# Attention and MLP on one core: the second layer of batches 2 and 3 as seven block products for two row tiles, with all sums on VectorE

## The chip, the cores and the metric

The kernel runs on one core of one Trainium2 chip. A core has TensorE (PE, matrix products, written to PSUM), VectorE (DVE), ScalarE (ACT), GpSimd (POOL) and SyncE (SP, which here only issues transfers), each with its own instruction queue that runs in order. The metric is device time in microseconds. Before the change three runs gave a median of 288.89 us (288.71 to 291.12).

## What is computed

```python
# q, k, v: (batch 4, heads 8, seq 768, head_dim 64), float32
k_chunks = k.reshape(B, H, 24, 32, D)                        # chunks of 32 keys
k_min, k_max = np.min(k_chunks, axis=3), np.max(k_chunks, axis=3)
ub = np.sum(np.maximum(q[..., None, :] * k_min, q[..., None, :] * k_max), axis=-1)
ub = np.where(causal_by_chunk, ub, -1e9)
top_chunks = np.argsort(ub, axis=-1)[..., -6:]               # each query keeps 6 chunks
scores = np.where(sel & causal, q @ k.T / sqrt(D), -1e9)
attn_out = softmax(scores) @ v
x = attn_out.transpose(0, 2, 1, 3).reshape(4, 768, 512)
xn = (x - mean(x)) / sqrt(var(x) + 1e-6) * g_ln              # over the last axis
out = x + np.maximum(xn @ w_ch1, 0.0) @ w_ch2                # 512 -> 2048 -> 512
```

So there is a chunk-selecting attention on each of 32 heads, then a layer norm, and a two-layer MLP with a residual on 3,072 rows.

## The kernel before

**Tiling.** Heads go in 16 pairs, `g` 0 to 15, four pairs to a batch. The 768 positions of a batch are six row tiles of 128; three row tiles make a half batch `(b, r)`. Attention works by pair (pairs 0 to 3 by pair and half batch), the MLP by half batch.

**Attention of a pair.** `ld`/`ldb` load keys and queries, `ldv` the values. `turn` transposes them (on PE for pairs 0 to 3, in blocks on DVE for the others). `kbound` takes each chunk's minimum and maximum (DVE), `kdiag` builds the right operand for the bounds (POOL from pair 4 on). `qhi`, `qlo`, `qrel` make the high and the low half of the scaled query and of its positive part, as float16 (ACT, DVE). `bounds` gives the upper bounds (PE), `select` finds the seventh largest of each row and makes a mask (DVE), `maskt` transposes it (PE), `mring` copies it from PSUM. The scores are one matmul whose operands hold the query or key of one head in 64 partitions and mask rows in the other 64. These operands lie in rings of four buffers, `QA`, `QB`, `KA`, `KB`. `kcopy` fills the key part. `qring` fills the query part: for pairs 0 to 3 by ACT out of PSUM, for pairs 4 to 15 by two transfers that SP issues (L267, L268). Then `smm` (scores, PE, L414), `sexp` (exponential, ACT, L422), `diag` (causal mask, POOL), `values` (PE, L445), `norm` and `pstat` (normalisation and statistics, DVE).

**MLP of a half batch.** `centre` (DVE, L487) writes `xc` = (x - mean) * g as float16. `rstd` puts 1/sqrt(var) aside, with the power on POOL. `xt` transposes `xc` by a transfer. `m1.b.r.m` is two of the sixteen hidden tiles of the first layer (PE, 8 matmuls of 384 columns, L513), `relu` takes them from PSUM to `hT` (ACT, in three places DVE). `m2.b.r.i.j` is a quarter of the second layer for row tile `i`: four of sixteen matmuls with `hT` as the weights and 512 columns of `w2b` (L538). `fin` multiplies by `rstd`, adds `x` (one DVE instruction, L547) and stores. The very last tile is split into 384 and 128 columns.

**Order.** One long list, `ORDER`, names every step; `fn.a.b@w` calls `fn(a, b)` with `w` in `other[0]`, which picks another engine or a number of keep-warm matmuls (`busy`, L117). Each engine runs its instructions in the order of that list. A step waits for its data, and for a buffer that it takes again: PSUM has four one-bank buffers (`ps_t`: transposes, bounds, values, second layer) and two of two banks (`ps_m`: scores and first layer).

The transfers all run on the core's 16 DMA engines; SP's queue issues in order, and POOL's issues the values and both weight matrices.

Of the kernel before, what the change touches and what calls it, by code (L numbers as in the profile page):

```python
# [19 lines left out]
def kernel(  # L20
# [10 lines left out]
    nc = tc.nc  # L31
# [228 lines left out]
    def qrel(g):  # L260
        qh, ql, rh, rl = (st[g][nm][:, P:] for nm in ("qh", "ql", "rh", "rl"))
        nc.vector.tensor_scalar_max(rh, qh, 0.0)
        nc.vector.scalar_tensor_tensor(rl, qh, 0.0, ql, op0=ALU.is_gt, op1=ALU.mult)

    def qring(g, i=None):
        if i is None:
# [71 lines left out]
    def select(g, i=None):  # L338
# [4 lines left out]
        if g >= HP:  # L343
            ubt = smp.tile([P, NT - 1, 2, NCH], F32, name="ubt", tag="ubt", bufs=1)
            ubm = smp.tile([P, NT - 1, 2, NCH], F32, name="ubm", tag="ubm")
            nc.vector.tensor_tensor(ubt, ub[:, :, 1], causf, ALU.add)
# [131 lines left out]

    def centre(b, r):
# [3 lines left out]
        for i in range(TR):  # L483
            nc.vector.bn_aggr(h["mv"][:, i, :], h["st"][:, i])
        for i in range(TR):
            xs = xh(b, r)[:, i].rearrange("p h d -> p (h d)")
            nc.vector.scalar_tensor_tensor(  # L487
# [39 lines left out]
    def last(b, r, i):  # L527
        return (b, r, i) == (B - 1, NR - 1, TR - 1)

    def m2(b, r, i, j):  # L530
# [3 lines left out]
        n, cs = 4, slice(0, DM)  # L534
        if last(b, r, i):
            n, cs = 8, slice(0, DM - P) if j < 2 else slice(DM - P, DM)
        for kt in range(n * j % KT2, n * j % KT2 + n):
            nc.tensor.matmul(  # L538
                h["yp", i][:, cs], h["hT"][:, kt, i * P:(i + 1) * P], w2b[:, kt, cs],
# [3 lines left out]
    def fin(b, r, i, e=None):  # L543
        h = hf[b, r]
        cs = (slice(0, DM), slice(0, DM - P), slice(DM - P, DM))[0 if e is None else 1 + e]
        ot = outp.tile([P, DM], F32, name="ot", tag="ot")
        nc.vector.scalar_tensor_tensor(  # L547
            ot[:, cs], h["yp", i][:, cs], h["rstd"][:, i:i + 1], xh(b, r)[:, i].rearrange("p h d -> p (h d)")[:, cs],
            op0=ALU.mult, op1=ALU.add,
        )  # L550
        s = TR * r + i
        nc.sync.dma_start(out[b, s * P:(s + 1) * P, cs], ot[:, cs])
# [4 lines left out]
        consts ld.0.0 rrows.0.0 rinit.0 ld.1.0 ld.2.0 warm.8 turn.0.qn.0 rrows.2.1@1 qpos.0.0 rrows.3.1 qring.0.0  # L557
        turn.0.kn.0 rinit.2 kbound.0.0 rinit.1 turn.1.qn.0 kcopy.0.0 ld.3.0 turn.1.kn.0 kbound.1.0 kdiag.0.0
        qring.1.0 rrows.1.0 rinit.3 turn.2.qn.0@3 ld.0.1 rrows.0.1 bounds.0.0@2 kdiag.1.0 rrows.1.1 qpos.1.0
        select.0.0 turn.2.kn.0 kcopy.2.0@1 kcopy.1.0 qpos.2.0 bounds.1.0@2 kbound.2.0 qring.2.0 maskt.0.0 select.1.0  # L560
# [130 lines left out]
```

## Time and profile before

| | us | share of the span |
|---|---|---|
| span of the profiled run | 288.7 | |
| PE busy | 271.7 | 94% |
| DVE busy | 211.8 | 73% |
| ACT busy | 180.8 | 63% |
| POOL busy | 94.1 | 33% |
| first layer on PE (L513), 512 matmuls | 87.9 | |
| second layer on PE (L538), 400 matmuls | 94.8 | |
| exponentials on ACT (L422) | 84.6 | |

Matmuls are pipelined, so the busy time of a row counts the latency of each, and rows overlap; how fast a stream of them runs is read from the chain of waits, where runs of equal matmuls stand with their total. The chain follows the work that ended last back from the end; PE holds 81% of it, DMA 8%, DVE 7%. The slices show when an engine was busy, and the windows give the same for chosen stretches. A DVE or ACT row's mean is the duration of one instruction.

### The profile page before, as it was taken

What the parts mean: (1) busy time and instruction counts of PE and PEld (TensorE: products, weight loads), DVE (VectorE), ACT (ScalarE), POOL (GpSimd) and SP (SyncE); (2) the same over time, 40 slices, a digit from 0 to 9 for tenths busy, and PEclk for the clock granted to TensorE, in tenths of its full rate; (3) what the DMA queues carried; (4) which work ended last, traced back from release to release, by engine and by line L of the source; (5) the groups of instructions that cost most, each with busy time, mean ns of one, the idle gap of its engine ahead of it and who ended that gap; (6) DMA issues with size and microseconds to landing.
All of it is one profiled execution on the core that took longest, in us unless ns stands there. A gap on an engine that the chain in (4) does not pass through costs nothing.

```text
span 288.7 us, 6793 instructions
## 1 busy us (share of the span) xinstructions
PE 271.7 (94%) x2628; PEld 181.8 (63%) x2628; DVE 211.8 (73%) x629; ACT 180.8 (63%) x241; POOL 94.1 (33%) x165
## 2 busy tenths in 40 slices
PE   5999999992799999999899999999999999999994
PEld 2889997671355777566656776566667745555541
DVE  5699999998079998999699979998797483221212
ACT  3688999694185977865775877667777522513210
POOL 8505615781039203182442643141072200100100
PEclk9999999998599999999999999999999999999999
DMA  6999997999949989489919691927011112310102
GB/s 141 203 179 177 202 156 126 167 151 194 139 84 70 188 162 182 78 116 133 172 29 185 112 148 20 136 81 163 16 43 59 39 20 72 93 39 36 73 0 110
DMA packets 136063, 32.42 MB, mean 112 GB/s; under 512 B 127072, under 2 KB 132960, under 8 KB 136032
## 3 DMA queue, kind: packets, MB, share of 16 engines
q1 hardware_dynamic: 106640, 24.39, 43.7%
q0 software_dynamic: 29248, 7.34, 27.4%
q8 instruction: 20, 0.33, 0.5%
q10 hardware_dynamic: 144, 0.26, 0.4%
q14 instruction: 11, 0.09, 0.1%
HBM read 27.53 MB, written 6.29 MB: 117 GB/s over the span
## 4 chain that ended last, share of the span: by engine, by line
PE 81%; DMA 8%; DVE 7%; ACT 2%; issue 1%; ACTq 0%; DVEq 0%
PE yp L538 27%; PE mm L513 25%; PE mm L414 11%; PE sm L445 6%; DMA QA<-q 3%; PE ub L333 3%; DMA xT<-xc 3%; PE ub L320 2%; ACT pt L422 2%; PE tr L236 2%; DMA raw<-in_k_dram 2%; PE tr L117 2%; DVE xc L487 1%; PE trh L361 1%; PE ub L117 1%; PE mm L117 1%
## 5 line engine op out<-in xcount | busy, mean ns | idle before, releaser
L422 ACT ACTIVATE pt<-mm 128x1024 f16<-128x1024 f32 (+2 forms) x96 | 84.6, 917 | 30.0 <-PE mm L414 28.9
L538 PE MATMUL yp<-w2b,hT 128*128 128x512 f16 (+2 forms) x400 | 94.8, 377 | 0.0
L513 PE MATMUL mm<-xT,w1b 128*128 128x384 f16 x512 | 87.9, 326 | 0.8 <-DMA xT<-xc 0.8
L525 ACT ACTIVATE hT<-mm 128x768 f16<-128x768 f32 x61 | 49.1, 810 | 59.0 <-PE mm L513 58.8
L513 PEld LDWEIGHTS <-w1b 128*128 128x128 f16 x512 | 49.5, 98 | 34.5 <-issue 0.9
L538 PEld LDWEIGHTS <-hT 128*128 128x128 f16 x400 | 38.0, 99 | 34.9 <-issue 2.1
L429 POOL TENSOR_SCALAR_AFFINE_SELECT pt<-pt 128x768 f16<-128x768 f16 x32 | 27.9, 878 | 46.6 <-ACT pt L422 46.6
L414 PE MATMUL mm<-QA,KA 128*128 128x128 f16 (+2 forms) x224 | 34.3, 248 | 8.4 <-DMA QA<-q 7.5
L547 DVE SCALAR_TENSOR_TENSOR ot<-yp,rstd,x 128x512 f32<-128x512 f32 (+2 forms) x25 | 17.9, 721 | 31.7 <-PE yp L538 18.5
L414 PE MATMUL mm<-QB,KB 128*128 128x128 f16 (+2 forms) x224 | 34.4, 248 | 0.0
L498 POOL TENSOR_TENSOR rstd<-ve,mhalf 128x3 f32<-128x3 f32 x8 | 7.0, 875 | 70.9 <-DVE ve L495 70.8
L414 PEld LDWEIGHTS <-KA 128*128 128x128 f16 x224 | 17.9, 98 | 16.5 <-DMA QA<-q 8.0
L445 PEld LDWEIGHTS <-pt 128*128 128x128 f16 x672 | 24.4, 98 | 2.3
L445 PE MATMUL sm<-va,pt 128*128 128x65 f16 x672 | 25.4, 193 | 0.0
L303 POOL TENSOR_TENSOR kc<-kc 128x24 f32<-128x24 f32 x12 | 6.2, 513 | 54.9 <-DVE kc L284 54.8
L414 PEld LDWEIGHTS <-KB 128*128 128x128 f16 x224 | 18.1, 99 | 4.4 <-issue 1.3
L475 DVE BATCH_NORM_STATS2 bst<-x 128x6 f32<-128x128 f32 x96 | 20.3, 276 | 0.0
L460 DVE TENSOR_TENSOR x<-sm,rden 128x384 f32<-128x384 f32 x32 | 17.8, 558 | 1.1
L256 DVE SCALAR_TENSOR_TENSOR q<-qnT,q 128x640 f16<-128x640 f32 x12 | 9.9, 828 | 10.1 <-ACT q L253 10.0
L487 DVE SCALAR_TENSOR_TENSOR xc<-x,mv,gall 128x512 f16<-128x512 f32 x24 | 16.7, 750 | 0.2 <-DMA xT<-xc 0.2
L206 POOL DMA_DIRECT2D va<-in_v_dram x12 | 12.8, 1064 | 0.0
L213 POOL DMA_DIRECT2D va<-in_v_dram x16 | 12.7, 795 | 0.0
(95 smaller groups left out, 347.8 us busy)
## 6 DMA issues: line engine op xcount, KB each, us to landing
out_dram<-ot SPq DMA_DIRECT2D x23, 256.0 KB, 2.3
qnb<-in_q_dram SPq DMA_DIRECT2D x48, 96.0 KB, 2.7
knb<-in_k_dram SPq DMA_DIRECT2D x48, 96.0 KB, 3.0
va<-in_v_dram POOLq DMA_DIRECT2D x12, 192.0 KB, 5.9
w1b<-in_moe_w_ch_dram POOLq DMA_DIRECT2D x4, 512.0 KB, 7.2
w2b<-in_moe_w_ch_dram POOLq DMA_DIRECT2D x4, 512.0 KB, 8.4
raw<-in_k_dram SPq DMA_DIRECT2D x16, 96.0 KB, 3.9
raw<-in_q_dram SPq DMA_DIRECT2D x16, 96.0 KB, 3.9
```

What stands on the lines that cost most here:

```text
L206: nc.gpsimd.dma_start(va[:, :, :, 0:D].rearrange("p h t d -> p (h t) d"), v[b, 2 * hp:2 * hp + 2].rearrange("h (t p) d -> p (h t) d", p=P),)
L414: nc.tensor.matmul(sc[:, hh, o:o + w * P], ks[:, t * P:(t + 1) * P], qs[:, s * P:(s + w) * P], start=True, stop=True,)
L422: nc.scalar.activation(st[g]["pt", r][:, 4 * i:4 * i + o].rearrange("p n h x -> p h n x"), st[g]["sc", r, i][:, :, 0:o * P].rearrange("p h ...
L429: nc.gpsimd.affine_select(out=dv, in_=dv, compare_op=ALU.is_ge, fill=0.0, base=0, pattern=[[0, 2 * TR], [1, P]], channel_multiplier=-1,)
L445: nc.tensor.matmul(pv[:, hh, s2, :], pt[:, where[t, s], hh, :], va[:, hh, t, 0:D + 1], start=(t == 0), stop=(t == s),)
L460: nc.vector.tensor_tensor(xh(b, r)[:, :, 2 * hp:2 * hp + 2, :].rearrange("p s h d -> p h s d"), pv[:, :, :, 0:D], rden.to_broadcast([P, 2, ...
L475: nc.vector.bn_stats(half(b, r)["st"][:, i, hp], xh(b, r)[:, i, 2 * hp:2 * hp + 2].rearrange("p h d -> p (h d)"),)
L487: nc.vector.scalar_tensor_tensor(h["xc"][:, i, :], xs, h["mv"][:, i, 0:1], gall, op0=ALU.subtract, op1=ALU.mult,)
L513: nc.tensor.matmul(hp_[:, i, 0:TR * P], w1b[:, kt, (m + i) * P:(m + i + 1) * P], h["xT"][:, kt], start=(kt == 0), stop=(kt == KT1 - 1),)
L525: nc.scalar.activation(h["hT"][:, m:m + 2], h["hp", m][:, :, 0:TR * P], ACTF.Relu, scale=HS)
L538: nc.tensor.matmul(h["yp", i][:, cs], h["hT"][:, kt, i * P:(i + 1) * P], w2b[:, kt, cs], start=(kt == 0), stop=(kt == KT2 - 1),)
L547: nc.vector.scalar_tensor_tensor(ot[:, cs], h["yp", i][:, cs], h["rstd"][:, i:i + 1], xh(b, r)[:, i].rearrange("p h d -> p (h d)")[:, cs], ...
```

## The change

The second layer of a pair of row tiles A and B is a product of a 2 x 2 block matrix with another: the rows are A and B, the inner blocks the lower and the upper half of the 2,048 hidden units, the columns the left and right half of the 512 outputs. Strassen's scheme, in Winograd's form, gives such a product by seven block products in place of eight, for sums of blocks before and after. The change does this for the twelve row tiles of batches 2 and 3, in six pairs.

- `tw`: four differences of blocks of `w2b`, once (DVE).
- `sc`: four sums or differences of blocks of `hT` for each pair (DVE).
- `sp.q.j`: product `j` of pair `q`, 8 matmuls of 256 columns.
- `sx`, `so`: the products' sums, added to `x` in place (DVE), and the stores from `x`.
- As the products of two row tiles are mixed, `rstd` is applied before the layers: for these batches `centre` calls `rstd` and takes two DVE instructions for a tile, and `fin` is left out.
- The query ring of pairs 4 and 5 is filled by engine copies in place of transfers; the order gives pair 4 to ACT (`qring.4@1`) and pair 5 to POOL (`qring.5@2`).
- `qrel`, `select` and `fin` get a second form on ACT and POOL, which the new order uses in places; it also uses the existing other forms of `kcopy`, `mring` and `relu` more often.
- The order is a new list throughout. It has 48 keep-warm matmuls of 240 columns at the scores and the first layer where there were 28, and 11 at the start where there were 8.

The aim is less work on PE, and no ring transfers while the loads of weights and values keep the DMA engines occupied.

```diff
     def qrel(g):
-        nc.vector.tensor_scalar_max(rh, qh, 0.0)
+        if other[0]:
+            nc.scalar.activation(rh, qh, ACTF.Relu)
+        else:
+            nc.vector.tensor_scalar_max(rh, qh, 0.0)
...
     def qring(g, i=None):
+        if HP <= g < HP + 2:
+            eng = pick(nc.vector, nc.scalar, nc.gpsimd)
+            copy(eng, QA[g % NK][0:64, :], st[g]["qh"][0:64, :])
+            copy(eng, QB[g % NK][64:P, :], st[g]["qh"][64:P, :])
+            return
...
     def select(g, i=None):
-            nc.vector.tensor_tensor(ubt, ub[:, :, 1], causf, ALU.add)
+            if other[0]:
+                nc.scalar.copy(ubt, ub[:, :, 1])
+                nc.gpsimd.tensor_tensor(ubt, ubt, causf, ALU.add)
+            else:
+                nc.vector.tensor_tensor(ubt, ub[:, :, 1], causf, ALU.add)
...
+    PAIRS = (
+        ((2, 1, 0), (2, 1, 1)), ((3, 0, 0), (3, 0, 1)), ((3, 1, 0), (3, 1, 1)), ((3, 0, 2), (3, 1, 2)),
+        ((2, 0, 0), (2, 0, 1)), ((2, 0, 2), (2, 1, 2)),
+    )
     def centre(b, r):
+        if (b, r) in UNIT:
+            rstd(b, r)
...
+                nc.vector.tensor_scalar(
+                    xn, xs, h["mv"][:, i, 0:1], h["rstd"][:, i:i + 1], op0=ALU.subtract, op1=ALU.mult,
+                )
+                nc.vector.tensor_tensor(h["xc"][:, i, :], xn, gall, ALU.mult)
...
     def fin(b, r, i):
+        if other[0]:
+            nc.scalar.activation(ot, y, ACTF.Copy, scale=scale)
+            nc.gpsimd.tensor_tensor(ot, ot, xs, ALU.add)
...
+    def tw(k):
+            a, c = {
+                1: lambda: (up[:, :, right], up[:, :, left]), 2: lambda: (low[:, :, right], tblocks(1, z, n)),
+                3: lambda: (low[:, :, right], up[:, :, right]), 4: lambda: (low[:, :, left], tblocks(2, z, n)),
+            }[k]()
+            eng.tensor_tensor(tblocks(k, z, n), a, c, ALU.subtract)
...
+    def sc(q, k):
+        o = s[k] = prp.tile([P, KH, P], F16, name=f"S{k}", tag=("T", "T", "q32", "r32")[k - 1])
+        if k == 1:
+            eng.tensor_tensor(o, hpart(Bt, 0), hpart(Bt, 1), ALU.add)
+        elif k == 2:
+            eng.tensor_tensor(o, s[1], hpart(A, 0), ALU.subtract)
+        elif k == 3:
+            eng.tensor_tensor(o, hpart(A, 0), hpart(Bt, 0), ALU.subtract)
+        else:
+            eng.tensor_tensor(o, hpart(A, 1), s[2], ALU.subtract)
+    def sp(q, j):
+        if j == 1:
+            s["y"] = ps_t.tile([P, 2, DH], F32, name="ya", tag="one")
+        if j == 6:
+            s["z"] = ps_t.tile([P, 2, DH], F32, name="yb", tag="one")
+        o = s["z"][:, 0] if j in (4, 6, 7) else s["y"][:, int(j in (3, 5))]
...
+    def sx(q, j):
+        src = s["z"][:, 0] if j in (6, 7) else s["y"][:, int(j == 5)]
+        if j in (1, 6):
+            more(A, src, slice(DH, DM))
+        if j == 1:
+            more(Bt, src, slice(0, DM))
+        if j in (5, 7):
+            more(Bt, src, slice(DH, DM))
+    def so(q, e):
+        if e == 0:
+            more(A, s["y"].rearrange("p c d -> p (c d)"), slice(0, DM))
+        else:
+            more(Bt, s["z"][:, 0], slice(0, DH))
+        store(*(Bt if e else A), rows(*(Bt if e else A)))
```

The end of the new order, where the last three pairs are worked:

```
        sc.3.2 relu.3.0.14 sp.3.1 sc.3.3 sx.3.1 m1.3.0.8 sp.3.6 sp.1.1 relu.3.0.8@1 sx.3.6 sc.2.3 sp.3.2 sp.2.1
        sc.3.4 sp.3.5 sx.1.1 sp.3.7 sc.1.1 sx.3.5 sp.1.2 sx.3.7 sp.3.3 sx.2.1 so.3.0 sp.1.5 sc.1.2 sp.2.2 sc.1.3
        sp.1.6 sp.3.4 sc.1.4 sx.1.6 sc.2.1 sp.1.7 so.3.1 sp.2.5 sc.2.2 sx.1.7 sx.1.5 sx.2.5 sp.2.6 sx.2.6 sc.2.4
        sp.1.3 so.1.0 sp.2.7 sx.2.7 sp.2.3 sp.2.4 sp.1.4 so.2.0 so.2.1 so.1.1
```

## The prediction, made before the changed kernel was run

> **What bounds the kernel now.** I read the 40 slices first, then the busy time by stretch, the chain of waits, the timeline of the DMA-issuing engine, and last the groups of instructions.
>
> ```profile
> PE   5999999992799999999899999999999999999994
> DVE  5699999998079998999699979998797483221212
> PEclk9999999998599999999999999999999999999999
> DMA  6999997999949989489919691927011112310102
> ```
>
> TensorE (PE) is full everywhere but at both ends and in slices 9 and 10 (one slice is 7.2 us), where its clock falls too. VectorE (DVE) is nearly full until slice 28 and then has room. DMA is full in the first ten slices.
>
> ```profile
> core 0: us, PE busy (x) PEld busy (x) DVE busy (x) ACT busy (x) POOL busy (x), PEclk, DMA share, GB/s
> ...
> 66.60:80.00 13.40, 5.91 (x23) 2.84 (x23) 4.42 (x14) 3.44 (x5) 0.00 (x0) 0.62 1.08 164
> 80.00:186.60 106.60, 105.84 (x1108) 69.44 (x1106) 97.25 (x272) 78.17 (x93) 41.09 (x69) 1.00 0.90 121
> 186.60:284.70 98.10, 98.06 (x792) 58.50 (x789) 50.73 (x138) 44.76 (x54) 14.61 (x22) 1.00 0.21 58
> ```
>
> In the hole no compute engine is busy and only DMA is (1.08). From 80 us on PE is without gaps, and DVE has 97.25 of 106.60 us. From 186.6 us, where the first layer of batch 2 begins, DVE has 47 us free.
>
> ```profile
> 64.57 9.57 DMA QA<-q
> ...
> 74.19 1.04 PE mm L414 x8
> 75.22 3.41 PE yp L538 x8
> ...
> 79.06 1.17 PE yp L538 x4
> ```
>
> The hole is one wait: the scores of pair 5 need the query ring (QA, QB), which a DMA fills. Afterwards PE runs at half clock: eight 512-column matmuls take 3.41 us, where four take 0.86 elsewhere on the chain, so 1.7 us are lost there, and 0.6, 0.2 and 0.3 us in the entries around it. The hole costs 7.5 us of waiting (the waits' own line) and 2.8 us of slow clock: 10.3 us.
>
> ```profile
> 59.85 4.60 SPq L194 DMA_DIRECT2D qnb<-in_q_dram  x4
> 64.57 3.00 SPq L267 DMA_DIRECT2D QA<-q  x1
> 67.67 1.24 SPq L268 DMA_DIRECT2D QB<-q  x1
> 69.72 4.78 SPq L504 DMA_TRANSPOSE xT<-xc  x3
> ```
>
> The ring copy of pair 5 is issued behind prefetches and lands 9.6 us later, beside weight loads. Its source had long been written.
>
> ```profile
> L538 PE MATMUL yp<-w2b,hT 128*128 128x512 f16 x368 | 91.3, 386 | 0.0
> ...
> L547 DVE SCALAR_TENSOR_TENSOR ot<-yp,rstd,x 128x512 f32<-128x512 f32 x23 | 17.1, 742 | 25.3 <-issue 12.8 <-PE yp L538 12.1 <-POOL rstd L498 0.3
> ```
>
> The second layer is a quarter of PE's work; its epilogue costs DVE 742 ns a tile. The 386 ns is a latency: on the chain 16 of these matmuls take 3.45 us, 216 ns each.
>
> [...] The chain agrees: 216 ns at 512 columns, 163 ns at 384 (16 in 2.60 us), 56 ns at 128 (8 in 0.45 us, each with its own weight load). I take 109 ns for 256 columns; the scores' 256-column pieces (four in 0.44 us) agree.
> [...] Here the clock read 0.50 from 70 to 78 us.
> [...] The trace confirms one per cycle (384 elements 558 ns, 240 elements 407 ns: about N/0.96 plus 157 ns). It has no 16-bit tensor_tensor; its 16-bit scalar_tensor_tensor ran at one (640 elements, 843 ns), its 16-bit copy out of PSUM at two (640 elements, 494 ns).
> [...]
>
> **The change, part by part.**
> *Second layer on PE.* Twelve row tiles in six pairs. Before, a pair takes 32 matmuls of 512 columns, 32 x 216 = 6.9 us. After, seven products of 8 matmuls of 256 columns, 56 x 109 = 6.1 us. Six pairs save 4.8 us. Weight loads rise from 32 to 56 a pair; the scores show one load and one matmul every 56 ns, so at 109 ns they stay hidden: 0.
>
> *DVE sums.* Input sums: 24 of 1,024 halves; at two a cycle 512/0.96 + 157 = 690 ns, at one 1.22 us. I take two[...]: 16.6 us (bound 29.3). Weight differences: four times 1,536 + 512 elements, 0.96 + 0.42 us: 5.5 us (bound 9.8). Output sums from PSUM: 12 of 512 at 690 ns and 30 of 256 at 423 ns: 21.0 us. The centring of the four half batches is now two instructions a tile (estimate 0.45 + 0.69 for 0.75): 12 x 0.39 = 4.7 us. Three more first-layer outputs on DVE at 958 ns: 2.9 us. Away: 18 of 23 epilogues and the two pieces of the last tile, 14.2 us; seven mask rings to ScalarE (ACT), 7 x 0.98 = 6.8 us; six maxima, four mask additions and small ones, some 5.2 us. Net +24.5: DVE goes from 211.8 to 236 us. From the first layer of batch 2 on I count 76 us (16.6 + 5.5 + 21.0, three centrings 12.8, five outputs 4.8, normalisation and statistics 10.9, two selections and the rest 4.3), against 50.7 before. PE there has 98.1 - 4.8 - 0.8 moved ahead = 92.5. So DVE is at 82%: beside PE, if the order feeds it well.
>
> *New waits.* A later product accumulates onto a PSUM half that a DVE sum has read, so within a pair PE waits for DVE three times. DVE is strictly in order; behind a late sum stand the next pair's input sums, and behind those PE. I walked the last three pairs by hand with 0.87 us a product and the durations above: PE needs 18.7 us of work and ends after 19.7. From the start of the first half batch of batch 3 in the first layer to the start of its other half, DVE has 16.5 of PE's 17.8 us, plus one wait for GpSimd (POOL) in the centring (0.88 us for the power, some 1.3 us round trip). Four such waits; behind each stand sums that PE needs much later, but for the one in batch 3. I book 1.0 us for the sums and waits together; end values 0 and 6.
>
> *Rings of pairs 4 and 5.* Despite the change's name the order sends them to ACT and POOL: two copies of 64x768 each, about 830 ns by the casts of the same size (KA<-knT). The POOL copy stands behind two loads' issues and the first two diagonals; by the times of before it runs from about 62 to 64 us, ahead of the scores at 66.6. So this wait goes. What then comes is the arrival of the second layer's weights: they were issued at about 60, 61.9 and 63.2 us and took 7.8 to 10.4 us to land. In the new order the pieces follow at about 61.5, 65 and 66.3, so they land at about 70, 73 and 74.5. PE wants the second at 68 and the third at 72: waits of 2 and 1 us[...]. Of 10.3 us I book 8.0 as gained (ends 4 and 10.3).
>
> *Fillers.* 20 more keep-warm matmuls of 240 columns, 2.05 us, in the attention of batch 0, where PE has some idle time (its instructions by form, times the stream price, leave 1.4 us open between 10 and 20 us and 1.7 us from there to 66 us). A third shows: +0.7 us (ends 0 and 2.1). Three more at the start lie in the wait for the first load: 0.
>
> *Work moved to ACT and POOL.* ACT gains some 8 us on 181 and POOL some 25 on 94[...]; neither reaches three quarters of the span. Hidden behind PE: 0. The end, sum and store, stays at about 4 us.
>
> Sum: 288.9 - 4.8 - 8.0 + 1.0 + 0.7 = 277.8 us.
>
> **The rivals.**
> *A. The hole moves to another transfer.* For it: DMA is at 1.08 to 1.16 of its share throughout the first 80 us, and the weights and the transposed activations are in the same queue. Against: DMA falls to 0.42 at 80 us, so the backlog is small. If only 2 us are gained: 288.9 - 4.8 - 2 + 1.7 = 283.8, with a second cold clock (2.8) 286.6.
> *B. DVE becomes the bound of the end.* 16-bit sums at one a cycle add 24 x 0.53 + 4 x 1.07 = 17.1 us: 93 us for PE's 92.5, without any wait between the two. With the 10% that DVE loses even in the dense stretch (97 of 107) this takes 103: 288.9 - 8.0 + 0.7 + (103 - 98.1) = 286.5; with a lumpy order or late rings on top, 290 to 297, slower than before. Against: the copy at two a cycle and the 82%.
> *C. Everything fits.* No new wait, fillers hidden: 288.9 - 4.8 - 10.3 = 273.8; with other small PE gaps of the first 66 us (3 us) closed, 271.
>
> **How the numbers follow.** The forecast (274 to 283) has 0.62, A (283 to 287) 0.15, B 0.13 (two thirds of it over 289), C (under 274) 0.10. The likeliest gives 277.8. The range 272.5 to 287.0 leaves out the worse part of B and the best of C, under 2 in 10. Faster by over 1% means under 286.0: the forecast, C, and two thirds of A, 0.82; within 1%: the rest of A and of B, 0.07; slower: 0.11.
>
> **What would show it.** Right: no wait for QA or QB near 66 us and a clock at 1.00 there; eight matmuls of 256 columns in 0.87 us; input sums of 1,024 at 0.6 to 0.7 us; PE without gaps over 0.5 us from 80 us on; DVE at about 80% from the first layer of batch 2. Wrong: PE waits for w2b or xT at 68 to 80 us (A), input sums at 1.2 us or many PE waits for DVE sums in the last 60 us (B). A long DVE wait for POOL in a centring, with PE waiting behind it, would break the step that books those at 1 us.

## The result, and the profile after

The changed kernel took 284.23 us (median of 4, 279.88 to 287.33), the kernel before, measured beside it, 288.80 (288.70 to 291.12). By the medians it is faster by 1.6%: inside the range that was given, but 6.4 us above the forecast of 277.8. In part of the executions of these kernels TensorE's mean clock is lower than in the rest (0.981 and 0.988 in two of these four, 1.000 and 0.999 in the others; 0.975 to 1.000 in 65 of the kernel before), so each median stands with its lowest and highest time, and is best compared with the medians of its own group. Here two executions took 279.88 and 281.40 us and two 287.06 and 287.33, just above the range. The median lies between them, where no execution was; 22 further executions, in the first group of experiments, have a median of 281.90.

In that group 15 of 65 executions of the kernel before took 280.2 to 286.3 us, the others 287.1 to 293.4. Its lowest, 280.20, is within 1 us of the lowest of the changed kernel, 279.25. So the change hardly moves the best execution; it makes a long one rarer. No profile of such a short execution of the kernel before was taken, so whether it lacks the wait at 66 us is not shown.

The slices of the changed kernel (one slice is 7.1 us):

```profile
PE   6999993999999999999999999799799999999994
DVE  4799989389999979998879998998979898856883
PEclk9999997899999999999999999999799999999999
```

The hole of slices 9 and 10 is gone. TensorE (PE) now has one in slice 6, at 43 to 50 us, with a low clock beside it, and a weaker one in slices 25 and 28. VectorE (DVE) stays well filled to the end, where before it had half its time free. The stretches show it, in us (in brackets the number of instructions):

```profile
core 0: us, PE busy (x) PEld busy (x) DVE busy (x) ACT busy (x) POOL busy (x), PEclk, DMA share, GB/s
40.00:52.50 12.50, 8.17 (x55) 5.56 (x52) 10.87 (x24) 5.87 (x9) 8.43 (x20) 0.74 1.16 156
66.60:80.00 13.40, 12.87 (x140) 8.21 (x140) 13.07 (x32) 11.36 (x15) 9.38 (x14) 1.00 0.88 128
160.00:210.00 50.00, 45.94 (x481) 30.15 (x478) 46.27 (x129) 38.68 (x54) 30.99 (x40) 0.97 0.56 91
210.00:285.60 75.60, 72.03 (x670) 56.23 (x666) 57.99 (x131) 24.59 (x30) 6.10 (x6) 1.00 0.17 53
```

From 66.6 to 80 us PE is busy for 12.87 of 13.40 us at full clock, where it was 5.91. From 210 us to the end it lacks only the last sum and store. What is new are the first row and the third.

The waits of PE, and two entries of the chain of waits, both of the changed kernel. A line of waits gives who waited, for what, the sum in us, the number and the longest:

```profile
PE mm L544 <- DMA xT<-xc: 4.3, 1, 4.3
...
PE mm L544 <- ACT ubt L355: 1.7, 1, 1.7
...
PE trh L373 <- DVE MN L364: 1.0, 1, 1.0
```

```profile
42.26 6.04 DMA xT<-xc
...
48.44 4.88 PE mm L544 x16
```

The queue that issues the transfers, near 44 us: first the kernel before, then the changed kernel, then another execution of the changed kernel, from the first experiment.

```profile
22.77 13.04 SPq L194 DMA_DIRECT2D knb<-in_k_dram  x8
38.18 4.13 SPq L504 DMA_TRANSPOSE xT<-xc  x3
```

```profile
26.82 12.65 SPq L194 DMA_DIRECT2D knb<-in_k_dram  x8
39.57 5.21 SPq L535 DMA_TRANSPOSE xT<-xc  x3
```

```profile
23.55 14.30 SPq L194 DMA_DIRECT2D knb<-in_k_dram  x8
37.96 3.89 SPq L535 DMA_TRANSPOSE xT<-xc  x3
```

Both orders ask for the keys of pairs 5 and 4, in eight issues, ahead of the transposes of the first half batch. In the kernel before these issues were through at 35.8 us, 2.4 us before the rows to transpose were ready. In the new order the rows are ready 1.8 us earlier and the eight issues start later, by 4.1 us in this execution and 0.8 in the other, so the issues now hold the transposes up. In this execution the last transpose also took 6.0 us from issue to landing (4.0 in the other, 4.4 before); why is not shown. It lands at 48.30, and the first layer waits 4.3 us for it. Then 16 matmuls take 4.88 us where they take 2.60 at full clock.

The groups that the change adds (line, engine, operation, tiles, shapes and count; busy time, mean ns; idle time before):

```profile
L646 PE MATMUL ya<-w2b,hT 128*128 128x256 f16 x96 | 11.9, 273 | 0.0
...
L516 DVE TENSOR_TENSOR xc<-xn,gall 128x512 f16<-128x512 f32 x12 | 9.4, 785 | 0.4
...
L655 DVE TENSOR_TENSOR x<-ya,x 128x512 f32<-128x512 f32 x12 | 8.2, 683 | 0.8 <-PE ya L646 0.8
L513 DVE TENSOR_SCALAR xn<-x,mv,rstd 128x512 f32<-128x512 f32 x12 | 7.9, 659 | 4.2 <-POOL rstd L529 3.9
...
L655 DVE TENSOR_TENSOR x<-yb,x 128x256 f32<-128x256 f32 x18 | 7.5, 419 | 2.5 <-PE yb L646 2.2
...
L625 DVE TENSOR_TENSOR S<-hT 128x1024 f16<-128x1024 f16 x6 | 4.1, 683 | 0.6 <-ACT hT L556 0.6
```

The sums cost what the prediction took (683 ns for 1,024 float16 values, 683 for 512 and 419 for 256 out of PSUM). For the first of these two a cycle was an estimate from one copy of before (640 values in 494 ns, some 0.53 ns a value beyond the 157 that the prediction takes as fixed); by the 683 ns it is 0.51. The two instructions of the centring cost more (659 and 785 ns, taken as 0.45 and 0.69 us), and DVE waits for GpSimd (POOL) for 3.9 us in all.

To see where PE's time goes I add up, for a stretch, its matmuls by form, each at the price at which a stream of it runs on the chains of waits (216 ns at 512 columns, 163 at 384, 109 at 256, 103 at 240 and 56 at 128, so about N/2.4 + 2.5 ns; for other widths that line is an estimate), and take the sum from the stretch's length. What is left is waiting or slow clock. The edges make this uncertain by some 0.5 us, and a few matmuls are missing from a trace. "Changed, again" is the execution from the first experiment.

| time that PE lost, us | span | 0–40 | 40–66 | 66–80 | 80–160 | 160–210 | 210–end |
|---|---|---|---|---|---|---|---|
| before | 288.7 | 9.9 | 1.3 | 9.9 | 0.4 | -0.3 | 4.0 |
| changed | 285.6 | 6.5 | 6.9 | 0.9 | -0.1 | 6.7 | 3.7 |
| changed, again | 279.8 | 6.5 | 2.2 | -0.1 | 0.3 | 5.8 | 3.4 |

The stream itself is 261.9 us before and 259.8 after: 4.8 less for the second layer, 2.7 more for keep-warm matmuls. The 3.4 us that the first column seems to gain are no gain: ahead of the first layer PE has the same matmuls in all three but for the fillers, and the first layer starts at 44.71 us before, at 44.76 in the second execution of the changed kernel and at 48.44 in the first. So those fillers fill waits. The hole gives 9 to 10 us back; 40 to 66 us takes up to 5.6 again, and 160 to 210 us takes 6 to 7.

### The profile page after: what moved, and what is told of

Same layout as the page of the kernel before. It is cut to its first block, busy times and chain, and to the rows that moved or that the text cites. A ratio compares the mean times of both kernels' runs of the same rounds, so it can differ in the third digit from the quotient of the medians.

```text
span 285.6 us, 7201 instructions
## 1 busy us (share of the span) xinstructions
PE 269.7 (94%) x2779; PEld 195.7 (69%) x2779; DVE 242.9 (85%) x670; ACT 186.7 (65%) x259; POOL 125.3 (44%) x194
## 4 chain that ended last, share of the span: by engine, by line
PE 73%; DVE 9%; DMA 6%; issue 4%; ACT 4%; SPq 2%; POOL 1%; DVEq 0%; POOLq 0%
PE mm L544 24%; PE yp L563 11%; PE mm L426 9%; PE ya L646 7%; PE yb L646 6%; PE sm L457 5%; ACT pt L434 2%; PE ub L341 2%; DMA xT<-xc 2%; PE tr L236 2%; DMA raw<-in_k_dram 2%; SPq L194 1%; PE tr L117 1%; PE ub L328 1%; DVE r L266 1%
## 5 line engine op out<-in xcount | busy, mean ns | idle before, releaser
L544 PE MATMUL mm<-xT,w1b 128*128 128x384 f16 x512 | 90.6, 334 | 6.2 <-DMA xT<-xc 4.3
L556 ACT ACTIVATE hT<-mm 128x768 f16<-128x768 f32 x58 | 46.6, 810 | 48.5 <-PE mm L544 43.1
L441 POOL TENSOR_SCALAR_AFFINE_SELECT pt<-pt 128x768 f16<-128x768 f16 x32 | 31.8, 1000 | 40.4 <-ACT pt L434 40.2
L563 PE MATMUL yp<-w2b,hT 128*128 128x512 f16 x192 | 47.8, 379 | 0.4 <-DVE x L472 0.3
L563 PEld LDWEIGHTS <-hT 128*128 128x128 f16 x192 | 17.9, 98 | 15.7 <-issue 0.8
L646 PEld LDWEIGHTS <-S 128*128 128x128 f16 x192 | 18.7, 98 | 2.8
L655 DVE TENSOR_TENSOR x<-ya,x 128x256 f32<-128x256 f32 (+1 forms) x24 | 12.6, 552 | 3.7 <-PE ya L646 3.6
L646 PEld LDWEIGHTS <-hT 128*128 128x128 f16 x144 | 14.0, 98 | 1.9
L581 POOL TENSOR_TENSOR ot<-ot,x 128x512 f32<-128x512 f32 x7 | 9.5, 1361 | 9.8 <-ACT ot L580 9.6
L229 DVE STREAM_TRANSPOSE knT<-knb 128x768 f32<-128x768 f32 x12 | 11.6, 965 | 1.8 <-ACT KB L112 1.1
L206 POOL DMA_DIRECT2D va<-in_v_dram x12 | 12.8, 1069 | 0.2
```

The source lines that it names most:

```text
L206: nc.gpsimd.dma_start(va[:, :, :, 0:D].rearrange("p h t d -> p (h t) d"), v[b, 2 * hp:2 * hp + 2].rearrange("h (t p) d -> p (h t) d", p=P),)
L441: nc.gpsimd.affine_select(out=dv, in_=dv, compare_op=ALU.is_ge, fill=0.0, base=0, pattern=[[0, 2 * TR], [1, P]], channel_multiplier=-1,)
L544: nc.tensor.matmul(hp_[:, i, 0:TR * P], w1b[:, kt, (m + i) * P:(m + i + 1) * P], h["xT"][:, kt], start=(kt == 0), stop=(kt == KT1 - 1),)
L556: nc.scalar.activation(h["hT"][:, m:m + 2], h["hp", m][:, :, 0:TR * P], ACTF.Relu, scale=HS)
L563: nc.tensor.matmul(h["yp", i], h["hT"][:, kt, i * P:(i + 1) * P], w2b[:, kt, :], start=(kt == 0), stop=(kt == KT2 - 1),)
L646: nc.tensor.matmul(o, lhs[:, kt], rhs, start=(kt == 0 and j in (1, 5, 6)), stop=(kt == KH - 1), skip_group_check=True,)
```

## The experiments

The kernels were measured in three groups of four, each beside the kernel before, which had medians of 289.70, 289.72 and 290.23 us. The first group has the changed kernel again, the rings alone, the rings by transfers and the keys behind the transposes. The second has the key copies on ACT, eight products, one-step centring and the first version with three pairs. The third has the spliced order, the split centring, the row scale on ACT and the second version with three pairs. Differences of a microsecond or two between medians of different groups mean little.

### The changed kernel again, and the rings alone

*The changed kernel unchanged*, for its spread and as the measure for the rest of its group.

> The changed kernel once more, for its spread and for a profile of another execution. In the profile at hand PE waits 4.3 us at 44 us for the transposed activations of the first half batch and then runs at half clock until 52.5 us. My theory: the wait lies at the edge of what drops the clock, so that executions differ by whether it does; where the clock holds I expect about 280 us and, at 40 to 60 us, 4 us less lost than the 6.2 us of this profile. Rival: the executions differ all over the span, and the stretch from 40 to 60 us looks the same.

Measured: 281.90 us (279.25 to 288.19, 22 executions), in two clusters: 14 at 279.3 to 282.3, eight at 286.5 to 288.2. The profile is of the first cluster:

```profile
core 0: us, PE busy (x) PEld busy (x) DVE busy (x) ACT busy (x) POOL busy (x), PEclk, DMA share, GB/s
40.00:52.50 12.50, 11.69 (x103) 8.44 (x101) 12.15 (x34) 9.88 (x15) 9.09 (x21) 1.00 1.03 145
160.00:210.00 50.00, 45.30 (x499) 31.06 (x498) 47.06 (x126) 39.35 (x54) 26.64 (x35) 1.00 0.39 76
```

```profile
PE mm L544 <- DMA xT<-xc: 0.7, 1, 0.7
```

With a wait of 0.7 us instead of 4.3 for the same transposes the clock stays at 1.00, and PE has 11.69 us of work there instead of 8.17. That is most of the 6 us between the clusters. The weak stretch from 160 to 210 us is in both.

*Only the rings of pairs 4 and 5*, by copies at the places of the old order (on DVE there; the new order names ScalarE (ACT) and POOL).

```diff
     def qring(g, i=None):   # in the kernel before
+        if HP <= g < HP + 2:
+            eng = pick(nc.vector, nc.scalar, nc.gpsimd)
+            copy(eng, QA[g % NK][0:64, :], st[g]["qh"][0:64, :])
+            copy(eng, QB[g % NK][64:P, :], st[g]["qh"][64:P, :])
+            return
```

> The kernel before with one edit: the query rings of pairs 4 and 5 are copied by DVE, at the places where their transfers were issued. My theory (the hole at 66 us is that transfer alone): the hole goes, 8 us gained less about 1 us for four DVE copies, so 280 to 282 us, ratio 0.97 to 0.975. Rival (the hole moves to the weights of the second layer, which land at about 70 us): 285 to 287 us.

Measured: 281.68 us (280.37 to 283.49, 18), a narrow spread. Its stretches:

```profile
160.00:210.00 50.00, 50.00 (x493) 32.13 (x492) 42.97 (x122) 36.73 (x44) 12.92 (x21) 1.00 0.47 84
210.00:279.00 69.00, 65.27 (x461) 36.76 (x457) 24.02 (x65) 20.90 (x26) 4.81 (x6) 0.99 0.16 52
```

PE lost 0.4 us from 66 to 80 us and nothing from 160 to 210, with DVE at 43 of 50 us. These five lines alone bring the whole gain of the changed kernel (281.68 against 281.90 us in the same group, and no execution above 283.5): the seven products, the new order and its fillers together add nothing to it.

*The changed kernel with the rings by transfers again* (the same block taken out).

> The changed kernel with one part undone: the rings of pairs 4 and 5 are filled by transfers again, at the new order's places. My theory: the transfer of pair 5 still lands late, PE waits 3 to 8 us between 64 and 75 us, 283 to 289 us. Rival (the new order, which issues that transfer ahead of both prefetches of pair 7, would have cured it without copies): as the changed kernel, 280 to 282 us.

Measured: 284.36 us (281.29 to 290.19, 22), 2.5 above the changed kernel. The wait for QA did not come back. The profile has the wait for the first transposes again, about as long as in the first profile of the changed kernel:

```profile
49.42 7.46 PE L539 MATMUL mm<-xT,w1b 128*128 128x384 f16 x32 [4.21 <-DMA xT<-xc]
```

The ring transfers can't have caused it, as they are issued after it, at 49.2 and 60.6 us. So in the new order they are early enough. The executions form two clusters here too, 12 at 281.3 to 284.4 us and 10 at 285.7 to 290.2; what the lower one has lost against 279.3 to 282.3 is not shown. The gain at 66 us has two sufficient causes: the copies in the old order, or the new order alone.

*The keys of pair 5 behind the transposes*, against the wait at 44 us.

```diff
-        sexp.3.0.1 ldb.5.kn ldb.4.kn pstat.1.0 ...
+        sexp.3.0.1 ldb.4.kn pstat.1.0 ...
-        xt.0.0.2 sexp.1.1.3 ...
+        xt.0.0.2 ldb.5.kn sexp.1.1.3 ...
```

> The changed kernel with the key prefetch of pair 5 issued behind the first three transposing transfers instead of ahead of them. My theory (the wait at 44 us comes from SP's queue, where those transfers are issued at 39.6 us though their source is ready at 37.7): the wait falls from 4.3 us to under 2, the clock holds in every execution, all times within 1% of each other, 277 to 280 us. Rival (the transfers are slow because all 16 DMA engines are full): the wait stays over 3 us and the times stay spread over 280 to 287.

Measured: 283.88 us (282.60 to 285.66, 14). The upper cluster is gone, but the lower one too, and the time missed what I expected. The transposes are issued earlier and PE no longer waits for them:

```profile
36.16 3.90 SPq L535 DMA_TRANSPOSE xT<-xc  x3
```

```profile
43.68 5.36 PE L544 MATMUL mm<-xT,w1b 128*128 128x384 f16 x32
...
55.93 1.94 PE L544 MATMUL mm<-xT,w1b 128*128 128x384 f16 x8 [2.00 <-ACT hT L556]
```

So the place of pair 5's keys in the queue is the cause of the wait at 44 us. But the keys that now come behind are missed:

```profile
48.39 0.98 DVE L229 STREAM_TRANSPOSE knT<-knb 128x768 f32<-128x768 f32 x1 [4.22 <-DMA knb<-in_k_dram]
```

DVE waits 4.22 us for them, ACT then waits for DVE's query transpose, its relu comes late, and PE waits 2.00 us for `hT`. The clock then reads 0.50 from 58 to 60 us (0.993 in the mean of the execution), and PE loses 5.1 us from 40 to 66. This order trades one wait for another.

### What fills 160 to 210 us

The DVE timeline of the changed kernel (start, length, instruction; in brackets the idle time before):

```profile
175.12 1.02 DVE L513 TENSOR_SCALAR xn<-x,mv,rstd 128x512 f32<-128x512 f32 x1 [0.98 <-POOL rstd L529]
176.18 1.19 DVE L516 TENSOR_TENSOR xc<-xn,gall 128x512 f16<-128x512 f32 x1
...
179.05 0.55 DVE L513 TENSOR_SCALAR xn<-x,mv,rstd 128x512 f32<-128x512 f32 x1
179.63 0.69 DVE L516 TENSOR_TENSOR xc<-xn,gall 128x512 f16<-128x512 f32 x1
...
202.82 0.47 DVE L364 TENSOR_TENSOR MN<-ubm,m 128x240 f16<-128x240 f32 x1
```

Two things stand in it: a wait of 0.98 us for the power, and instructions that take nearly twice as long beside two POOL casts (1.02 and 1.19 us, against 0.55 and 0.69 at 179 us, where POOL runs nothing). Both lengthen: `xc`, which reads two tiles (1.19 against 0.69), and `xn`, which reads one tile and two columns of scalars (1.02 against 0.55). What in the casts does it is not shown. The mask of the last line ends the chain of pair 14's selection, and PE waits 1.04 us for it at 203.3.

What stands behind each centring is the point. Behind the first of batch 2 stand its own transposes, the last issued at 180.3 us, and the first layer starts on them after a wait of 1.74 us at 184.8. The list of waits puts that wait to ACT's `ubt`; the profiles of the two kernels above (rings by transfers, keys behind the transposes) have a wait of 1.9 us for `xT` at the same place. Behind the second stands the selection of pair 14. With the centring in one instruction, below, both waits are gone.

*The key copies of pairs 13 to 15 on ACT instead of POOL.*

```diff
-        kcopy.13@1 ... kcopy.14@1 ... kcopy.15@1
+        kcopy.13 ... kcopy.14 ... kcopy.15
```

> The changed kernel with the two key copies of pairs 13, 14 and 15 on ScalarE instead of GpSimd. It tests why the stretch from 160 to 210 us loses about 8 us of TensorE time in the changed kernel, while the kernel before with only the ring copies loses none there. Theory ([...]VectorE is the bound of that stretch): some 5 us less GpSimd work between 160 and 185 us, the query subtraction and selection of pairs 14 and 15 back from 1.3 to about 0.85 us each, TensorE's loss from 160 to 210 us smaller by 1.5 to 3 us, and a time of 279.5 us (lower group of executions near 279). Rival (VectorE's own amount of work, or ScalarE, is the bound there): the lengths may drop but the loss stays, or the 5 us that ScalarE gets delay its exponentials and relus; then 282 to 284 us.

Measured: 288.08 us (286.79 to 293.96, 6): 6 us above the changed kernel's 281.90 in the other group, and the profile is of the highest execution. DVE's `xn` fell from a mean of 771 to 637 ns in this stretch and `xc` from 876 to 793, but PE lost 11.9 us instead of 5.8 (the second execution of the changed kernel). ACT's timeline shows why:

```profile
182.21 0.83 ACT L112 CAST KA<-knT 64x768 f16<-64x768 f32 x1 [2.81 <-DVE knT L229]
```

ACT waits 2.81 us for DVE's transpose, and the exponentials behind it in its queue come late; PE waits 4.3 us for them (`pt`) between 176 and 206 us, and 2.5 for a PSUM buffer that they free. The rival holds: the lengths drop, the queue costs more.

*Eight products again in the new order.* Each `sp.q.j` becomes four matmul steps of one of its two row tiles, `so` becomes `fin`, and `sc`, `sx`, `tw` go. The lines of the order are shown as a scheme.

```diff
-        sp.q.1 sx.q.1 sp.q.6 sp.q.2 sp.q.5 sx.q.6 sp.q.7 sx.q.5 sp.q.3 so.q.0 sp.q.4 so.q.1
+        m2.A.0        m2.B.0 m2.A.1 m2.A.2        m2.B.1        m2.A.3 fin.A  m2.B.2 m2.B.3 fin.B
-    UNIT = {t[:2] for pair in PAIRS for t in pair}
+    UNIT = set()   # one-instruction centring, rstd after it
```

> The changed kernel, in its new order and with its ring copies, but with the second layer of batches 2 and 3 by eight block products again: each block product of the order stands for four of the sixteen steps of one of its two row tiles (the last for eight), the input sums, weight differences and partial output sums are left out, the centring is one instruction per row tile and the row scale is applied in the last sum. Theory (the seven products save 4.8 us of TensorE, but their sums fill VectorE and the stretch from 160 to 210 us gives the gain back): VectorE falls from 244 to about 218 us, TensorE's ideal time rises by 4.8, its loss from 160 to 210 us falls from 8 to about 3, and the time is the same within 1.5 us, 281 to 283 (about 282 in the lower group). Rival (the seven products are worth their full 4.8 us, and the loss in that stretch comes from the new order alone): 286.5 us. Second rival (the sums cost more than the products save): under 279 us.

Measured: 285.54 us (283.38 to 291.08, 6), 3.6 above the changed kernel's 281.90; the medians are of different groups, but the lowest times differ by 4.1 too. My theory that the seven products net nothing falls: they are worth some 3 to 4 of their 4.8 us within this order. By the profiles the stream grows by 4.8, and the loss from 160 to 210 us falls only from 5.8 to 2.6, although DVE is busy there for just 37.20 us of 50. In that stretch PE waits 1.1 us for causal masks of POOL and 0.7 for exponentials of ACT. So the new order itself costs something against the old, some 4 us by the medians of this kernel and the rings alone, again of different groups. The two profiles differ by 4.9 us: 3.0 are lost from 160 to 210 us, 1.2 from 66 to 80, 0.6 from 80 to 160. The fillers and the first column cancel, and the rest is within the error of the sums.

*Centring in one instruction*, with the row scale of batches 2 and 3 left out.

```diff
-        if (b, r) in UNIT:
-            rstd(b, r)
...
-            if (b, r) in UNIT:   # xn, then xc
+            if False:
```

> The changed kernel with the seven products and all their sums, but the centring of batches 2 and 3 by one instruction per row tile and without the row scale, so that no wait for GpSimd's power stands in VectorE's queue; the row scale of batches 2 and 3 is left out altogether. Theory: two waits of 1.0 us, twelve instructions of 0.66 to 1.09 us less and four of the small GpSimd powers less, so 8 to 9 us of VectorE, about 4 of them in the stretch from 170 to 200 us: TensorE's loss there falls by 2 to 4 us and the time to 278.5 us. Rival (the two-step centring lies beside other waits; the sums of the products fill the stretch): no change, 281.5 to 282.5 us.

Measured: 281.32 us (276.93 to 284.04, 6). In its profile the loss from 160 to 210 us is 1.7 us instead of 5.8, with the products and all their sums still there:

```profile
160.00:210.00 50.00, 48.87 (x576) 33.83 (x574) 44.91 (x127) 43.03 (x59) 31.77 (x42) 1.00 0.63 97
```

So about 4 us of that stretch come from the two-instruction centring and its wait: 4.6 us of `xn` and 2.0 of waiting stand there in the changed kernel. The load of DVE alone doesn't order these losses: it is busy for 44.9 us of the 50 here and PE loses 1.7, for 43.0 with the rings alone and PE loses nothing, for 37.2 with eight products and PE loses 2.6. The times show no gain of 4 us (281.32 against 281.90, of different groups). The profiled execution, the highest, has the wait at 44 us (8.4 us lost from 40 to 66), and by their clocks (0.988 to 0.994 in four of six) others may have lost time there too. The lowest, 276.93 at a clock of 1.000, is 2.3 under the lowest of the changed kernel.

### Old front, new back

Both orders have done the same steps after their first 437 entries, near 100 us, but for three keep-warm matmuls at the start, so they can be spliced there.

```diff
+ORDER = before's first 437 entries, then the changed kernel's from 438 on
```

> The changed kernel with the first 437 entries of its order taken from the order before: both orders have done exactly the same work at that place, near 100 us, so this is the old order in front and the new one, with the seven products, behind. Theory (two separate causes: the new front order brings the wait for the transposed centred rows near 44 us in part of the executions, the new back order and the two-step centring cost 5 to 8 us from 160 to 210 us): the wait near 44 us and the clock drop are gone, the executions spread over 3 us instead of 9, TensorE's loss from 160 to 210 us stays at 5 to 8 us, and the time is 280.5 us. Rival (the front of the new order itself gains or loses more than the wait): the work that TensorE has done by 100 us differs from the ring copies alone, and the time moves to 278 or 283 us accordingly.

Measured: 284.50 us (282.38 to 285.22, 6). The wait at 44 us is gone and the spread is 3 us, as the theory had it; the loss from 160 to 210 us stays, 5.8. But the time is 4 us above what I expected. Four of the six ran with a mean clock of 0.988 to 0.994, the two near 282.4 with 0.998 and 1.000. The executions without the clock loss are near the changed kernel's lower cluster (279.3 to 282.3, of another group). A profile of an execution with the loss was not taken for this kernel; in that of the next one the clock is at half from 199 to 202 us, within the same stretch.

*The centring split*, so that the power is asked for earlier.

```diff
+    def stat(b, r):     # bn_aggr and rstd, right after the last pstat
...
     def centre(b, r):   # xn, xc at the old place
```

> The old front and the new back as in the run beside it, and the centring of batches 2 and 3 in two parts: mean, variance and the GpSimd power right after the last row statistics, the two instructions per row tile at their old places, with other VectorE work between them. No work is added or left out; the wait of VectorE for the power alone goes. Theory: two waits of 1.0 us leave the stretch from 170 to 200 us and two the tail, and of these 2 to 3 us 1 to 2 reach the end: 279 us, 1 to 2 below the run beside it. Rival (the amount of work on VectorE, not the wait, bounds the stretch): under 0.5 us of difference.

Measured: 284.10 us (282.18 to 285.62, 6): no difference from the 284.50 of the spliced order. But the waiting was not taken away. The lines of POOL, of the issuing queue and of DVE for the second centring of batch 2:

```profile
187.56 1.34 POOL L534 TENSOR_TENSOR rstd<-ve,mhalf 128x3 f32<-128x3 f32 x1 [1.60 <-DVE ve L531]
```

```profile
190.18 0.36 SPq L578 DMA_DIRECT2D out_dram<-ot  x1
```

```profile
192.31 1.00 DVE L518 TENSOR_SCALAR xn<-x,mv,rstd 128x512 f32<-128x512 f32 x1 [2.44 <-POOL pt L441]
```

The power is done at 188.9 us, so the wait for it has shrunk to 0.3 us, but `xn` starts only at 192.3. The view names POOL, which had long been done. `xn` takes one of the two buffers that the outputs of `fin` use, and the store from one was issued at 190.18 and landed some 2 us later; by these times the 2.44 us were a wait for that buffer. In all DVE waits 2.7 us in this stretch instead of 2.0. The run can't tell the wait from the work; how the 4 us of the centring divide stays open.

*The row scale on ACT.*

```diff
+    def unit(b, r):     # just ahead of the transposes
+        for i in range(TR):
+            nc.scalar.activation(h["xc"][:, i, :], h["xc"][:, i, :], ACTF.Copy, scale=h["rstd"][:, i:i + 1])
-            if (b, r) in UNIT: xn, then xc
```

> The old front and the new back, with the centring of batches 2 and 3 by one VectorE instruction per row tile as in batches 0 and 1, and the row scale applied to its 512 values by ScalarE. VectorE gets 12 instructions of 0.66 us and its waits for GpSimd less, ScalarE 12 of about 0.5 us more, each behind a wait for the power. Theory (the two-step centring on VectorE takes 3 to 4 us from the stretch from 160 to 210 us, as the kernel without it showed): 277.5 us, if ScalarE's exponentials are not held up by the scaling. Rival (ScalarE, whose queue is in order, waits for the power and the exponentials behind it come later, as with the key copies on ScalarE): no gain, 281 us or more.

Measured: 293.73 us (291.23 to 295.52, 6), the highest median of all. ACT's and PE's timelines:

```profile
191.04 1.95 ACT L515 ACTIVATE xc<-xc,rstd 128x512 f16<-128x512 f16 x3 [7.22 <-POOL rstd L524]
```

```profile
193.73 6.29 PE L539 MATMUL mm<-xT,w1b 128*128 128x384 f16 x24 [7.47 <-ACT hT L551]
```

ACT stood for 7.22 us at the head of its queue for a power that depends on DVE's backlog. The relus behind it came late, and PE stood 7.47 us for the buffer that they free.

### Seven products where DVE has room

*Old order, ring copies, and only the three pairs of batch 3 by seven products*, in the tail, where DVE is busy for 1.4 to 6 of every 10 us in the run with the rings alone. In this version product 5 of one pair is begun between its products 1 and 2, and part of the output is left out. That it is product 1, in the left half of row tile A, is the author's estimate; no trace shows it.

```diff
-    UNIT = {t[:2] for pair in PAIRS for t in pair}
+    UNIT = {(3, 0), (3, 1)}
+ORDER = before's up to centre.3.1, then a new tail with tw.1 to tw.4 between its steps and:
+  m1.3.1.12 relu.3.1.12 sp.2.1 sc.2.1 sc.2.2 sx.2.1 sp.2.5 sp.2.6 ... m1.3.0.0 sp.2.2 ...
```

> The kernel before with the ring copies of pairs 4 and 5 on VectorE and its own order up to the last centring but one, and then only the three pairs of row tiles of batch 3 by seven block products, in a tail close to that of the changed kernel. In the kernel with the ring copies alone VectorE is busy 1.4 to 6 of every 10 us from 220 us on, so the 25 us of sums and weight differences of three pairs fit there, and TensorE lost nothing from 160 us on. Theory (seven products pay where VectorE has room): three pairs by 0.8 us, 2.4 us less than the ring copies alone, so 279.3 us, with a narrow spread. Rival (the sums hold up the tail: input sums after the last relu and sums between products of one bank stand on the path): 281.5 to 285 us.

Measured: 283.32 us (281.41 to 284.60, 6), no better than the rings alone (281.68, of the first group). PE's timeline:

```profile
245.59 1.04 PE L646 MATMUL ya<-w2b,hT 128*128 128x256 f16 x8
249.03 1.38 PE L646 MATMUL ya<-tw,S 128*128 128x256 f16 x8 [2.41 <-DVE x L655]
250.21 1.91 PE L646 MATMUL yb<-tw,S 128*128 128x256 f16 x8
```

After the last relu, two input sums and an output sum stand on DVE, and PE waits 2.41 us for them; then its clock is at half until 253 us (eight products take 1.91 us instead of 1.04). PE lost 8.7 us from 210 us on, against 3.8 with the rings alone.

*The same with two first-layer pieces between the first product and the sums, and both products of one half of the accumulator ahead of the other half's.*

```diff
-  ... sp.2.1 sc.2.1 sc.2.2 sx.2.1 sp.2.5 sp.2.6 sc.2.4 sc.2.3 tw.4 sx.2.5 sx.2.6 m1.3.0.0 sp.2.2 ...
+  ... sp.2.1 m1.3.0.0 sx.2.1 sc.2.1 relu.3.0.0 sp.2.2 m1.3.0.12 sc.2.2 relu.3.0.12 tw.4 sp.2.5 sp.2.6 ...
```

> The three pairs of batch 3 by seven block products behind the old order, as before, with two first-layer pieces moved between the first product and the sums that the next products of the pair need, so that TensorE has 2.6 us of other work where it lost 3.9 us, and with the two products of one half of the accumulator before those of the other. Theory: the hole near 247 us closes and the time is 278.5 to 279.5 us, 2.4 below the ring copies alone. Rival (the sums of the last two pairs still stand on the path after the last relu): 280.5 us or more.

Measured: 278.66 us (278.48 to 279.57, 6): the lowest median of all kernels here and the narrowest spread, 5.8 under the spliced order of the same group. Its slices and stretches:

```profile
PE   6899999999999999999999999999999998999994
PEclk9999999999999999999999999999999999999999
```

```profile
160.00:210.00 50.00, 50.00 (x492) 32.00 (x491) 43.02 (x122) 36.80 (x44) 13.77 (x22) 1.00 0.47 84
210.00:276.00 66.00, 62.17 (x511) 42.56 (x509) 45.20 (x104) 19.56 (x24) 3.98 (x5) 1.00 0.16 53
```

PE is full from 160 to 210 us, the clock falls in no slice, and DVE has taken 45 us of work behind 210 us instead of 24. Three pairs at 0.8 us are 2.4 us; the medians differ by 3.0 from the rings alone (another group). Beside little POOL work its `xn` took 546 ns and `xc` 693.

| time that PE lost, us | span | 0–40 | 40–66 | 66–80 | 80–160 | 160–210 | 210–end |
|---|---|---|---|---|---|---|---|
| rings alone | 279.1 | 9.7 | 2.6 | 0.4 | -0.3 | -0.4 | 3.8 |
| eight products, new order | 284.0 | 6.8 | 2.7 | 1.6 | 0.3 | 2.6 | 4.0 |
| one-step centring | 282.3 | 6.5 | 8.4 | 0.8 | -0.1 | 1.7 | 3.5 |
| key copies on ACT | 292.0 | 6.5 | 7.9 | 0.9 | -0.2 | 11.9 | 4.2 |
| old front, new back | 280.7 | 9.2 | 2.3 | 0.5 | 0.7 | 5.8 | 3.5 |
| row scale on ACT | 290.0 | 9.3 | 1.9 | 0.4 | 1.0 | 14.1 | 4.5 |
| three pairs, mended tail | 276.6 | 8.7 | 2.2 | 0.5 | 0.0 | -0.4 | 4.5 |

## Why the prediction was right and where it was not

- **Faster, and by which cause.** Right in sign, and the larger of the two gains that it named carries it: the rings alone reach 281.68 us. All the rest was forecast at -3.1 us net (-4.8 for the products, +1.0 and +0.7) and measured at nothing: 281.90 against 281.68 in the same group. The range held because the term of the rings was sound and the range wide. That the first median, 284.23, fell inside it and not above was partly luck, as two of its four executions lay at 287.1 and 287.3. That median lies in the interval of rival A, the 281.90 of 22 executions in the interval of the forecast.
- **The hole, booked at 8.0 of 10.3 us.** No wait for QA or QB is left at 66 us and the clock reads 1.00 there, as it was to show. PE's loss there fell by 9 to 10 us, so the term was rather too small. The waits for `w2b` that I set against it did not come (0.3 us at most).
- **Rival A, a hole that moves.** It came, for a part of the executions, but at 44 us and not at 68 to 80. I read the issuing queue only around the old hole. The eight key issues stood ahead of the transposes in the old order too, with 2.4 us to spare; that the new order uses this up was not priced. It costs 5.6 us where it comes (6.9 against 1.3 us lost from 40 to 66).
- **Second layer, 4.8 us.** The price per product held, eight matmuls in 0.87 us:

```profile
211.76 0.87 PE ya L646 x8
```

  Loads stayed hidden. What reached the end is some 3 to 4 us within the new order (times of two groups).
- **Sums and new waits, 1.0 us (ends 0 and 6).** This is the term that failed: PE lost 5.8 to 6.7 us from 160 to 210 us, where it lost nothing before. The sums had the right price. Two steps were wrong. The first is that behind each of the four waits in a centring, but for the one in batch 3, stand only sums that PE needs much later. In batch 2 its own transposes and pair 14's selection stand behind them, and PE waited 1.7 and 1.0 us for these. The second is to judge DVE by its mean from the first layer of batch 2 to the end (82%). The load isn't even: pairs 13 to 15 are prepared early in the new order, and the centring of the two halves of batch 2 falls beside them, so DVE has 46 to 47 of 50 us in this stretch. The centring was priced at 1.14 us a tile and cost 1.44. With the centring in one instruction PE lost 1.7 us there. How much of the rest is the wait and how much the work is not shown.
- **"PE without gaps over 0.5 us from 80 us on"** failed in the same stretch: waits of 1.7 and 1.0 us.
- **DVE's total of 236 us** was 242.9. The centring gives 3.6 us of the difference (12 x 0.30), and two groups that I took at their old lengths 3.3 (`q` L256 986 instead of 828 ns, the mask L364 580 instead of 462, twelve each), both beside more POOL work.
- **"Work moved to ACT and POOL: hidden, 0."** POOL's share of the span stayed low (44%), but its work beside DVE is not free: DVE's instructions were longer beside it, by the rows above (`xn` 1.02 us for 0.55). By how much that alone moves the end was not isolated: taking the key copies off POOL shortened DVE and cost more on ACT.
- **Fillers, 0.7 us.** Those ahead of 40 us cost nothing that is seen: the first layer starts at 44.76 us in the second execution of the changed kernel, 44.71 before. What the later ones cost was not isolated.
- **Rival B, the end bound by DVE.** Refuted: PE lost 3.7 us behind 210 us, 4.0 before, with DVE at 58 of 76 us. **Rival C, everything fits**, needed both the wait at 44 us and the stretch at 160 us away; no profiled execution of the changed order had that. The lowest execution with one-step centring, 276.93 us, may have come near it, but has no profile.
- **What stays open:** what in the new order makes it lose 3.0 us from 160 to 210 us even with eight products, beyond the 1.8 us of waits named there, and 1.2 from 66 to 80; and how the centring's 4 us divide between work and wait.

## What to carry to other kernels

Before a large change to an order, try its smallest part alone: here five lines that replace four transfers by copies bring what the whole change brings. Trade one engine's time for another's only where the profile by stretch, not by span, shows room: three pairs in the loose tail gained, the six pairs with their new order did not, though the products themselves were worth 3 to 4 us within it. Before you call a wait harmless, list what stands behind it in that engine's queue: here it was not only the sums but the transposes and a mask. Work moved to a third engine in an in-order queue brings its waits along, and they hold up everything behind it: on ACT 2.81 us for the transpose behind a key copy and 7.22 us for the power behind a row scale.

## What was not expected of the hardware

- Short waits too were followed by a lower clock. Single waits of 0.7 us (changed kernel, second execution), 1.74 (changed kernel), 1.91 (rings by transfers) and 1.93 (keys behind the transposes) left it at 1.00; waits of 2.00 us (keys behind the transposes), 2.41 (three pairs, first version) and 4.3 were each followed by 0.50. So were several small gaps: after 0.31, 0.31, 0.17 and then 1.04 us for the mask it read 0.50 at 204 to 206 us in the changed kernel, while much the same gaps left it at 1.00 in its second execution and in the spliced order. Of the waits of 2 and 1 us that the prediction expected at 68 to 72 us the first is as long as the shortest single wait here that was followed by 0.50; that the clock would hold over both was the author's estimate.
- Some DVE and POOL instructions took up to a little over two times as long beside each other. In the changed kernel `xn` took 0.55 us with POOL idle, 1.02 beside a cast and 1.09 beside a causal mask, `xc` 0.69, 1.19 and 1.23. At 197 to 200 us, beside POOL's small steps for the bounds, `xn` and `xc` kept 0.55 and 0.72 us, and POOL's cast of the bounds took 0.60 us, for 0.26 at 186.4.
